# Sliding-window attention and a gated linear unit on one core: a rewrite with a fixed instruction order, 1 KB input rows and wider instructions

## The chip, the cores and the metric

The kernel runs on one core of a Trainium2 chip. The metric is the device time in microseconds of one execution, from the first to the last instruction of the core. The kernel before was timed three times: 296.49 us is the median, 295.57 and 297.37 are the ends. The profile shown here is a separate, recorded execution, whose span is 296.8 us.

## What is computed

There are 8 batches, 8 heads, 576 positions and 64 elements per head. Each position attends to at most 32 keys: heads 0 to 3 to the last 32 positions ("plain"), heads 4 to 7 to every fourth of the last 128 ("dilated"). The heads are joined to 512 channels, and a gated linear unit with a causal convolution of five taps follows.

```python
def _attn_ref(q, k, v):
    B, H, S, D = q.shape                      # 8, 8, 576, 64
    window, dilation = 32, 4
    scores = (1.0 / np.sqrt(D)) * np.matmul(q, k.transpose(0, 1, 3, 2))
    rel = pos[:, None] - pos[None, :]
    mask_plain = (rel >= 0) & (rel < window)
    mask_dil = (rel >= 0) & (rel < window * dilation) & (rel % dilation == 0)
    ...                                        # plain for h < H // 2, else dilated; softmax
    return np.matmul(attn, v)

def _moe_ref(x, w_val, conv_w, w_out):         # x: [8, 576, 512]
    ...                                        # xp: x with 4 zero rows ahead of each batch
    for k in range(K):                         # K = 5
        gate_pre += conv_w[k][None, None, :] * xp[:, k:k + S, :]
    gate = 1.0 / (1.0 + np.exp(-gate_pre))
    return gate * (x @ w_val) @ w_out
```

## The kernel before

Two heads make a pair, and a batch has four pairs, two plain and two dilated; 32 pairs in all. For each pair the kernel loads q, k and v, transposes q and k on TensorE (reading the upper halves of the fp32 words as bf16), computes the scores of blocks of 72 or 96 queries against 128 keys, takes the exponential on ScalarE, multiplies by a mask on VectorE, multiplies by v (with a column of ones that gives the sum), normalises, and transposes the result into `xT`, channels on partitions. The gated unit works on groups of 512 columns of `xT` and is put between the pairs. A scheduler orders the instructions of each engine.

```python
    # loads: one 256-byte row (64 fp32) per position and head
    for name, src in (("q", q), ("k", k)):
        t = inbuf.tile([KT, NKT, HPC, D], FP32, name=f"{name}_nat")      # KT = 96, NKT = 6, HPC = 2
        for hh in range(HPC):
            nc.sync.dma_start(out=t[:, :, hh, :],                          # line 186
                in_=src[b, h].rearrange("(t p) d -> p t d", p=KT))
    ...                                   # v, plain: three loads; dilated: eight loads, line 213

    # attn_pair
    for kt in range(NKT):
        nc.tensor.transpose(out=ps[:, kt * KT:(kt + 1) * KT],             # line 237
                            in_=src[:, kt, :, :], identity=ident_b[0:KT, 0:KT])
    if name == "q": nc.scalar.copy(out=dst, in_=ps)                       # line 244
    else:           nc.vector.tensor_copy(dst, ps)                        # line 246
    ...
    for grp in groups:                    # two halves of the blocks
        for hh in range(HPC):
            ps = ps_main.tile([128, 512], FP32, name="ps1")
            for bi in grp:
                nc.tensor.matmul(out=ps[0:klen, col:col + qlen],          # line 269
                    lhsT=kT[rb:rb + D, ucols(klo, klen, dil)],
                    rhs=qT[rb:rb + D, ucols(qlo, qlen, dil)], start=True, stop=True)
            nc.scalar.activation(out=et2[:, hh, g0:g0 + gcols],           # line 276
                in_=ps[:, 0:gcols], func=AF.Exp, scale=scale)
            nc.vector.tensor_tensor(out=et2[...], in0=et2[...],           # line 280
                in1=mask[:, g0:g0 + gcols], op=ALU.mult)
        for hh in range(HPC):
            for ci, bi in enumerate(grp):
                nc.tensor.matmul(out=ps[0:qlen, ci * AVS:ci * AVS + D + 1],   # line 288
                    lhsT=et2[0:klen, hh, offs[bi]:offs[bi] + qlen],       # 72 or 96 columns
                    rhs=v_bf[0:klen, bi, hh, 0:D + 1], start=True, stop=True)
            nc.vector.reciprocal(out=rec[0:QB, 0:na], in_=xv[0:QB, :, D])     # line 298
            nc.vector.tensor_tensor(out=xn[...], in0=xv[...], in1=rec[...])   # line 299
    ...                                   # transposes of xn, line 308
    if not dil: nc.vector.tensor_copy(dst_cols, xt_ps)                    # line 315
    else:       nc.vector.tensor_copy(dst_ap, src_ap)                     # line 323, written with a step of 4

    # gated unit: 10 groups of up to 512 columns, 4 channel blocks each
    def moe_group(c, grp):
        for kk in range(K):   nc.tensor.matmul(...)                       # line 331, conv_diag, 5 taps
        nc.scalar.activation(out=gate, in_=psg, func=AF.Tanh, scale=0.5)  # line 338
        for mc in range(NCH): nc.tensor.matmul(...)                       # line 342, w_val
        nc.vector.scalar_tensor_tensor(out=y_all[...], ...)               # line 348
    def moe_out_tile(b, t):               # five tiles of 128 (the last 64) positions per batch
        for c in range(NCH):  nc.tensor.matmul(...)                       # line 359, w_out
        nc.scalar.copy(out=osb, in_=pso)                                  # line 366
        nc.scalar.dma_start(out=out[b, bs0:bs0 + blen, :], in_=osb)
```

Of the kernel before, what the change touches and what calls it, by code (L numbers as in the profile page):

```python
# [24 lines left out]
def kernel(  # L26
# [10 lines left out]
    nc = tc.nc  # L37

# [3 lines left out]
    window = 32  # L42
    dilation = 4
    seg = S // dilation
    scale = 1.0 / float(D) ** 0.5

    KT = 96
    NKT = S // KT
    DT = seg // 2

    NCH = Dm // 128
    HPC = 128 // D
    NG = H // HPC

    SB = S + 4
    CB = B * SB
    GP = 512
    NGR = _ceil_div(CB, GP)

    KW = 128  # L60
    plain_blocks = []
    for t in range(NKT):
        qlo = t * KT
        klo = max(0, min(qlo - window, S - KW))
        plain_blocks.append((klo, KW, qlo, KT))
    dil_blocks = []
    for r in range(dilation):
        for x in range(2):
            qlo = r * seg + x * DT
            klo = max(r * seg, min(qlo - window, (r + 1) * seg - KW))  # L70
            dil_blocks.append((klo, KW, qlo, DT))

    def flat_offsets(blocks):
        offs, tot = [], 0
        for (_, _, _, qlen) in blocks:
            offs.append(tot)
            tot += qlen
        return offs, tot

    plain_offs, plain_tot = flat_offsets(plain_blocks)  # L80
    dil_offs, dil_tot = flat_offsets(dil_blocks)
    ET_COLS = max(plain_tot, dil_tot)
    NT_MAX = max(len(plain_blocks), len(dil_blocks))

    def head_cfg(dil):
        if dil:
            return dil_blocks, dil_offs, dil_tot, DT
        return plain_blocks, plain_offs, plain_tot, KT

    consts = ctx.enter_context(tc.tile_pool(name="consts", bufs=1))  # L90
    glob = ctx.enter_context(tc.tile_pool(name="glob", bufs=1))
    inbuf = ctx.enter_context(tc.tile_pool(name="inbuf", bufs=4))
    work = ctx.enter_context(tc.tile_pool(name="work", bufs=4))
    etbuf = ctx.enter_context(tc.tile_pool(name="etbuf", bufs=4))
    moe_sb = ctx.enter_context(tc.tile_pool(name="moe_sb", bufs=4))
    outbuf = ctx.enter_context(tc.tile_pool(name="outbuf", bufs=3))

    ps_tr = ctx.enter_context(tc.tile_pool(name="ps_tr", bufs=2, space=bass.MemoryType.PSUM))
    ps_main = ctx.enter_context(tc.tile_pool(name="ps_main", bufs=6, space=bass.MemoryType.PSUM))
    ps_moe = ps_main  # L100
    ps_sc = ps_main
    ps_av = ps_main

    ident_b = consts.tile([128, 128], BF16)
    nc.gpsimd.memset(ident_b, 0.0)
# [342 lines left out]
```

The softmax here doesn't subtract the row's maximum and nothing guards it: scores larger than these inputs give would overflow.

## Time and profile before

| engine | busy, us | share of the span | instructions |
|---|---|---|---|
| TensorE matmul | 219.5 | 74% | 2028 |
| TensorE weight load | 130.5 | 44% | 2028 |
| VectorE | 168.1 | 57% | 544 |
| ScalarE | 108.6 | 37% | 245 |
| GpSimd | 9.3 | 3% | 50 |

The core read 35.66 MB from memory and wrote 9.44 MB. The mean granted clock of TensorE was 0.853 of full speed. The busy time of an engine is what of the span one or more of its instructions cover. Where instructions overlap in the pipeline, the durations add up to more than the time they cover, so the pace of a run of matmuls is read from the distance between their starts. In the tables "x" is a count, and the text behind a bar names the idle time ahead of the group and what ended it.

### The profile page before, as it was taken

To read this page: it belongs to the slowest core of one execution; us is meant where nothing else is said; L and a number is where in the kernel's file an instruction comes from. 1 tells how busy PE (TensorE), PEld (TensorE's weight loads), DVE (VectorE), ACT (ScalarE), POOL (GpSimd) and SP (SyncE) were. 2 spreads that over 40 slices of the span, in tenths; PEclk is the share of its full clock that TensorE was granted. 3 is DMA by queue.
4 is the path that set the end of the run, shared out by engine and by line. 5 is a ranking of instruction groups with operands and counts; after the bars stand their busy time and mean duration, and the time that the engine had idled before them with its cause. 6 is when DMAs were issued, how large, how long until landed. Compare 5 with 4: busy or idle time off the path is not lost.

```text
span 296.8 us, 5724 instructions
## 1 busy us (share of the span) xinstructions
PE 219.5 (74%) x2028; PEld 130.5 (44%) x2028; DVE 168.1 (57%) x544; ACT 108.6 (37%) x245; POOL 9.3 (3%) x50
## 2 busy tenths in 40 slices
PE   1136559765798759785988488975978598879994
PEld 1125445454445445543555344543554355534441
DVE  0295666565647665765676464764576655655310
ACT  2022223422235522452345333542255225542253
POOL 9300000000000000000000000000000000000000
PEclk9999999955589958995799659995899559989998
DMA  7998899898500599749975699559975996540035
GB/s 207 253 176 174 149 203 161 182 205 156 93 0 35 161 207 181 151 150 177 202 153 148 168 208 155 130 156 195 192 147 175 175 190 121 160 111 0 2 141 177
DMA packets 142277, 45.47 MB, mean 153 GB/s; under 512 B 136613, under 2 KB 136613, under 8 KB 142250
## 3 DMA queue, kind: packets, MB, share of 16 engines
q1 hardware_dynamic: 135936, 33.57, 66.9%
q10 hardware_dynamic: 6314, 11.55, 11.2%
q8 instruction: 16, 0.26, 0.4%
q14 instruction: 11, 0.09, 0.1%
HBM read 35.66 MB, written 9.44 MB: 152 GB/s over the span
## 4 chain that ended last, share of the span: by engine, by line
PE 52%; DVE 14%; DMA 13%; SPq 13%; ACT 4%; issue 3%; DVEq 0%; ACTq 0%
PE ps L331 15%; PE ps L342 12%; PE ps L359 7%; DMA k_nat<-in_k_dram 6%; PE ps L288 6%; SPq L186 6%; PE ps L269 5%; DVE xT L323 4%; DMA out_dram<-out_sb 4%; SPq L213 4%; PE tr_ps L237 4%; DVE kT L246 4%; DVE y_all L348 3%; PE tr_ps L308 3%; SPq L205 2%
## 5 line engine op out<-in xcount | busy, mean ns | idle before, releaser
L288 PE MATMUL ps<-v_nat,et 128*72 128x65 bf16 (+1 forms) x448 | 50.0, 234 | 16.2 <-DVE et L280 15.3
L331 PE MATMUL ps<-xT,conv_diag 128*128 128x512 bf16 (+2 forms) x200 | 61.1, 406 | 0.0
L276 ACT ACTIVATE et<-ps 128x288 bf16<-128x288 f32 x128 | 42.2, 415 | 43.8 <-PE ps L269 43.8
L288 PEld LDWEIGHTS <-et 128*72 128x72 bf16 (+1 forms) x448 | 40.1, 147 | 37.3 <-DVE et L280 29.7
L280 DVE TENSOR_TENSOR et<-et,mask_flat 128x288 bf16<-128x288 bf16 x128 | 37.7, 299 | 30.5 <-ACT et L276 30.5
L348 DVE SCALAR_TENSOR_TENSOR y_all<-gate,ps 128x512 bf16<-128x512 bf16 (+2 forms) x40 | 25.3, 637 | 35.7 <-PE ps L342 30.1
L299 DVE TENSOR_TENSOR x_norm<-ps,recip 72x256 bf16<-72x256 f32 (+1 forms) x128 | 45.2, 376 | 0.2
L342 PE MATMUL ps<-xT,w_val_b 128*128 128x512 bf16 (+2 forms) x160 | 44.1, 386 | 0.4 <-DVE xT L323 0.4
L338 ACT ACTIVATE gate<-ps 128x512 bf16<-128x512 f32 (+2 forms) x40 | 22.2, 556 | 57.5 <-PE ps L331 57.5
L359 PE MATMUL ps<-w_out_b,y_all 128*128 128x512 bf16 (+1 forms) x160 | 42.1, 381 | 0.0
L244 ACT COPY qT<-tr_ps 128x576 bf16<-128x576 bf16 x32 | 20.4, 638 | 50.5 <-PE tr_ps L237 50.5
L269 PE MATMUL ps<-qT,kT 64*128 64x72 bf16 (+1 forms) x448 | 20.7, 244 | 20.1 <-DVE kT L246 17.7
L366 ACT COPY out_sb<-ps 128x512 f32<-128x512 f32 (+1 forms) x40 | 23.4, 585 | 27.2 <-PE ps L359 17.7
L237 PE MATMUL tr_ps<-ident_b,k_nat 96*128 96x96 bf16 x192 | 16.4, 233 | 19.5 <-DMA k_nat<-in_k_dram 9.7
L308 PE MATMUL tr_ps<-ident_b,x_norm 72*128 72x72 bf16 (+1 forms) x224 | 23.6, 228 | 8.9 <-DVE v_nat L192 8.3
L298 DVE RECIPROCAL recip<-ps 72x4 f32<-72x4 f32 (+1 forms) x128 | 20.9, 172 | 15.5 <-PE ps L288 13.3
L323 DVE COPY xT<-tr_ps 128x576 bf16<-128x576 bf16 x16 | 23.1, 1444 | 8.7 <-PE tr_ps L308 8.7
L269 PEld LDWEIGHTS <-kT 64*128 64x128 bf16 x448 | 15.0, 116 | 25.4 <-DVE kT L246 24.3
L246 DVE COPY kT<-tr_ps 128x576 bf16<-128x576 bf16 x32 | 14.6, 456 | 20.2 <-PE tr_ps L237 20.2
L308 PEld LDWEIGHTS <-x_norm 72*128 72x128 bf16 (+1 forms) x224 | 16.3, 112 | 21.3 <-DVE v_nat L192 11.0
L331 PEld LDWEIGHTS <-conv_diag 128*128 128x128 bf16 x200 | 18.7, 108 | 14.8 <-issue 3.3
L237 PE MATMUL tr_ps<-ident_b,q_nat 96*128 96x96 bf16 x192 | 17.0, 235 | 7.9 <-DMA q_nat<-in_q_dram 7.8
(26 smaller groups left out, 83.9 us busy)
## 6 DMA issues: line engine op xcount, KB each, us to landing
q_nat<-in_q_dram SPq DMA_DIRECT2D x64, 144.0 KB, 3.9
k_nat<-in_k_dram SPq DMA_DIRECT2D x64, 144.0 KB, 4.3
v_nat<-in_v_dram SPq DMA_DIRECT2D x144, 64.0 KB, 2.9
out_dram<-out_sb ACTq DMA_DIRECT2D x32, 256.0 KB, 2.2
v_nat<-in_v_dram SPq DMA_DIRECT2D x32, 160.0 KB, 4.1
w_stage<-in_moe_w_val_dram ACTq DMA_DIRECT2D x1, 1024.0 KB, 6.6
w_stage<-in_moe_w_out_dram ACTq DMA_DIRECT2D x1, 1024.0 KB, 10.6
out_dram<-out_sb ACTq DMA_DIRECT2D x8, 128.0 KB, 2.3
```

The costliest lines, as they stand in the source:

```text
L237: nc.tensor.transpose(out=ps[:, kt * KT:(kt + 1) * KT], in_=src[:, kt, :, :], identity=ident_b[0:KT, 0:KT],)
L269: nc.tensor.matmul(out=ps[0:klen, col:col + qlen], lhsT=kT[rb:rb + D, ucols(klo, klen, dil)], rhs=qT[rb:rb + D, ucols(qlo, qlen, dil)], st ...
L276: nc.scalar.activation(out=et2[:, hh, g0:g0 + gcols], in_=ps[:, 0:gcols], func=AF.Exp, scale=scale,)
L280: nc.vector.tensor_tensor(out=et2[:, hh, g0:g0 + gcols], in0=et2[:, hh, g0:g0 + gcols], in1=mask[:, g0:g0 + gcols], op=ALU.mult,)
L288: nc.tensor.matmul(out=ps[0:qlen, ci * AVS:ci * AVS + D + 1], lhsT=et2[0:klen, hh, offs[bi]:offs[bi] + qlen], rhs=v_bf[0:klen, bi, hh, 0:D ...
L299: nc.vector.tensor_tensor(out=xn[0:QB, b0:b0 + na, hh, :], in0=xv[0:QB, :, 0:D], in1=rec[0:QB, 0:na, None].to_broadcast([QB, na, D]), op=A ...
L308: nc.tensor.transpose(out=xt_ps[:, bi * QB:(bi + 1) * QB], in_=xn[0:QB, bi, :, :], identity=ident_b[0:QB, 0:QB],)
L323: nc.vector.tensor_copy(dst_ap, src_ap)
L331: nc.tensor.matmul(out=psg[:, lo:glen], lhsT=conv_diag[:, c, kk, :], rhs=xT[:, c, g0 + lo + kk - (K - 1):g0 + kk - (K - 1) + glen], start= ...
L342: nc.tensor.matmul(out=psv[:, lo:glen], lhsT=w_val_b[:, mc, c * 128:(c + 1) * 128], rhs=xT[:, mc, g0 + lo:g0 + glen], start=(mc == 0), sto ...
L348: nc.vector.scalar_tensor_tensor(out=y_all[:, c, g0 + lo:g0 + glen], in0=gate[:, lo:glen], scalar=1.0, in1=psv[:, lo:glen], op0=ALU.add, o ...
L359: nc.tensor.matmul(out=pso[0:blen, 0:Dm], lhsT=y_all[:, c, b * SB + 4 + bs0:b * SB + 4 + bs0 + blen], rhs=w_out_b[:, c, :], start=(c == 0) ...
```

## The change

The kernel is rewritten; what is computed stays. The order of the instructions of each engine is now the order of the program text, with no scheduler. The aims are fewer and larger DMA packets, fewer and longer instructions on VectorE and ScalarE, weight loads of always 128 columns, and matmuls of the gated unit placed where TensorE would wait.

- q and k (and v of dilated pairs) come in rows of four positions (1 KB). So a partition holds positions 4p to 4p+3, one of each residue class.
- Dilated pairs: each transpose takes two classes of one head (128 columns), still read as the upper bf16 halves. v is cast to bf16 on GpSimd.
- Plain pairs: GpSimd casts q and k to bf16 in the order class, head, element; eight transposes each follow. k is put back in position order by a ScalarE copy that reads PSUM with a step of 144 elements. q stays in class order.
- Scores of both heads go to two neighbouring PSUM banks; one exponential, one mask multiply, one reciprocal and one normalising multiply take both.
- The copy to `xT` goes to ScalarE for all pairs, and reads PSUM with the same step.
- `et` and `kT` are padded so that a weight load always takes 128 columns.
- Groups of the gated unit no longer run over the padding between batches; a group that crosses a batch border is done in two pieces. The output tiles are 36 of 128 positions.
- Weights come by a casting DMA of GpSimd, after the loads of the first pairs.

The core of the diff, cut:

```diff
+    ctx.enter_context(tc.manual_schedule(engines=None))
...
+    ps_s = ctx.enter_context(tc.tile_pool(name="ps_s", bufs=2, space=bass.MemoryType.PSUM))
+    ps_m = ctx.enter_context(tc.tile_pool(name="ps_m", bufs=4, space=bass.MemoryType.PSUM))
...
+        for name, src in (("q", q), ("k", k)):
+            rows = src[b, 2 * g:2 * g + 2].rearrange("h (p r) d -> p h (r d)", r=R)
+            a = inbuf.tile([P0, 2, R * D], FP32, name=f"{name}a")
+            nc.sync.dma_start(out=a, in_=rows[0:P0])
...
+    def convert(i):
+        if is_dil(i):
+            a, z, c0, c1 = nat[i]["v"]
+            for src, dst in ((a, c0), (z, c1)):
+                nc.gpsimd.tensor_copy(
+                    dst[:, :, :, 0:D], src.rearrange("p h (r d) -> p h r d", r=R))
+        else:
+            for name in ("q", "k"):
...
+                    nc.gpsimd.tensor_copy(
+                        c.rearrange("p r h d -> p h r d"),
+                        src.rearrange("p h (r d) -> p h r d", r=R))
...
+        if name == "k" and not is_dil(i):
+            nc.scalar.copy(out=dst[:, 0:S].rearrange("p (t r) -> p t r", r=R),
+                           in_=ps[:, 0:S].rearrange("p (r t) -> p t r", r=R))
+        else:
+            nc.vector.tensor_copy(dst[:, 0:S], ps[:, 0:S])
...
+        ps = ps_s.tile([128, 2, 512], FP32, name="sc")
...
+        nc.scalar.activation(out=et[:, :, 0:HALF], in_=ps[:, :, 0:HALF],
+                             func=AF.Exp, scale=scale)
...
+        nc.vector.tensor_tensor(out=ev, in0=ev, in1=for_mask, op=ALU.mult)
...
+                    nc.tensor.matmul(out=ps[:, x, c * DA:(c + 1) * DA],
+                                     lhsT=et[:, x, c * 96:c * 96 + 128],
+                                     rhs=vb[:, 3 * hf + c, x, :], start=True, stop=True)
...
+        nc.scalar.copy(out=xT[:, g, c0:c0 + S].rearrange("p (t r) -> p t r", r=R),
+                       in_=pv.rearrange("p r t -> p t r"))
...
+    groups = [(512 * j, 512) for j in range(7)] + [(3584, 448), (4032, 320), (4352, 256)]
...
+    def load_w(dst, src):
+        nc.gpsimd.dma_start(out=dst, in_=src.rearrange("(c p) n -> p c n", p=128))
...
+    COST = {"C": 1.1, "V": 0.9, "O": 0.9}
...
+    def fill(share):
+        budget[0] += share
+        while queue and budget[0] > 0.0:
+            budget[0] -= COST[queue[0][0]]
+            run_item()
...
+    transpose_in(0, "q")
+    transpose_in(0, "k")
+    per = 3.2
+    for i in range(n_steps):
+        b, g = order[i]
+        if i + 2 < n_steps:
+            load_qk(i + 2)
+            load_v(i + 2)
+            convert(i + 2)
+        if i == 0:
+            load_w(w_val_b, moe_w_val)
+        if i == 2:
+            load_w(w_out_b, moe_w_out)
+        scores(i, 0)
+        scores(i, 1)
+        fill(per * 0.35)
+        attn_v(i, 0)
+        if i + 1 < n_steps:
+            transpose_in(i + 1, "q")
+            transpose_in(i + 1, "k")
+        attn_v(i, 1)
+        fill(per * 0.65)
+        transpose_x(i)
+        if i < NCH:
+            conv_consts(i)
+        if i % NG == NG - 1:
+            for gi in group_ready.get(b, []):
+                add_group(gi)
+    while queue:
+        run_item()
```

In the new kernel a "step" is one pair. A unit of the gated unit is C (five convolution matmuls and a tanh), V (four value matmuls and the product) or O (four output matmuls, a copy and a store). `fill` takes units from a queue until a budget of 3.2 per step is used up.

## The prediction

> **What bounds the kernel now.** I read the page's slices first, then the windows of one batch, then the chain that ended last, then the groups.
>
> The slices (forty of 7.4 us; rows are busy tenths, granted TensorE clock, DMA share):
>
> ```profile
> PE   1136559765798759785988488975978598879994
> DVE  0295666565647665765676464764576655655310
> PEclk9999999955589958995799659995899559989998
> DMA  7998899898500599749975699559975996540035
> ```
>
> TensorE is never idle for long and never steadily full, its clock falls to half again and again, and the DMA engines go from nine tenths to nothing and back. It is a pattern with a period of 32 us, one batch. Four windows of 8 us show one period (matmul, weight load, VectorE, ScalarE, GpSimd busy with counts, granted clock, DMA share, GB/s):
>
> ```profile
> 104.00:112.00 8.00, 5.11 (x48) 3.54 (x49) 5.19 (x17) 1.96 (x5) 0.00 (x0) 0.50 1.27 207
> 112.00:120.00 8.00, 7.33 (x50) 3.83 (x48) 4.44 (x13) 2.43 (x4) 0.00 (x0) 0.87 1.08 171
> 120.00:128.00 8.00, 7.17 (x85) 4.49 (x86) 5.55 (x22) 4.39 (x12) 0.00 (x0) 1.00 0.70 148
> 128.00:136.00 8.00, 6.16 (x67) 3.56 (x66) 5.47 (x18) 4.16 (x9) 0.00 (x0) 0.91 0.48 147
> ```
>
> In the first window the DMA queues are full (207 GB/s), TensorE works 5.1 of 8 us, and all of it at half clock. Only in the other windows does TensorE run near full, with full clock. The chain says the same (share of the span by what it ran through):
>
> ```profile
> PE 52%; DVE 14%; DMA 13%; SPq 13%; ACT 4%; issue 3%; DVEq 0%; ACTq 0%
> ...
> 53.14 0.86 PE ps L342 x4
> 54.00 1.07 PE ps L331 x5
> ...
> 134.43 0.77 PE ps L288 x8
> 136.56 3.66 DMA k_nat<-in_k_dram
> ...
> 157.09 0.73 PE ps L269 x16
> ```
>
> So no one engine is the bound: half the span is TensorE work, a quarter is loads and their issue, the rest is hand-overs to VectorE. The chain also gives paces: a 512-column matmul takes 0.215 us (1.07/5, 0.86/4), a score matmul 0.73/16 = 0.045 us, a matmul with v 0.77/8 = 0.096 us. Six input transposes started 0.26 us apart from the next six at 87.4 us, 0.043 us each. The groups with the shapes kept apart give the weight loads and VectorE's costs:
>
> ```profile
> L288 PEld LDWEIGHTS <-et 128*96 128x96 bf16 x192 | 20.6, 160 | 18.8 <-DVE et L280 14.6 <-issue 3.1
> L269 PEld LDWEIGHTS <-kT 64*128 64x128 bf16 x448 | 15.0, 116 | 25.4 <-DVE kT L246 24.3 <-issue 1.2
> L323 DVE COPY xT<-tr_ps 128x576 bf16<-128x576 bf16 x16 | 23.1, 1444 | 8.7 <-PE tr_ps L308 8.7
> L280 DVE TENSOR_TENSOR et<-et,mask_flat 128x288 bf16<-128x288 bf16 x128 | 37.7, 299 | 30.5 <-ACT et L276 30.5
> L276 ACT ACTIVATE et<-ps 128x288 bf16<-128x288 f32 x128 | 42.2, 415 | 43.8 <-PE ps L269 43.8
> ```
>
> A load of 96 columns takes longer than one of 128, and a copy with a stepped output 1444 ns where the contiguous one of the same size takes 458.
>
> [...] 160 ns for 96 columns, 116 for 128. [...] the load queue's 135,936 packets, nearly all of 256 B, took 66.9% of 16 x 296.8 us, 23.4 ns each or 10.9 GB/s per engine; the other queue's 6,314 (11.55 MB) took 11.2%, 84 ns for 1,829 B on average, 21.8 GB/s. [...] Here 64 elements more cost the normalising multiply 63 ns (345 at 192, 408 at 256), so about 155 ns of each are fixed. [...]
>
> **The change part by part.**
>
> DMA. Before: 66.9% and 11.2% of the span, 232 us of all 16 engines. After: q and k 2 x 32 x 288 = 18,432 rows of 1 KB, dilated v 16 x 2 x 176 = 5,632; at an estimated 45 ns (half of the 84 ns, a little more) 24,064 x 45 / 16 = 68 us. Plain v stays at 24,576 of 256 B: 36 us. Output and weights 5,632 x 84 / 16 = 30 us. Sum 134 us, 100 less. At a step of under 6 us this is 4.2 us per step, no longer what one waits for. The load wait of some 3.5 us in each batch, and the half-clock window it makes, should go.
>
> VectorE, with the fixed cost: q copies 32 x 456 ns = 14.6 us; k copies of dilated pairs 16 x 456 = 7.3; mask multiplies 64 x (299 + 150) = 28.7; reciprocals 64 x 180 = 11.5; normalising 32 x 659 + 32 x 533 = 38.1; products 36 x 688 = 24.8; diagonals 3.3. Sum 128 us against 168. The largest single item is the copy to `xT` (23.1 + 7.3) that leaves.
>
> ScalarE gets it: exponentials 64 x (415 + 240) = 42; tanh 36 x 597 = 21.5; outputs 36 x 586 = 21; copies 48 x 638 = 31 if a stepped read costs no more than a contiguous one; stores some 13 us of issue. Sum 128 us against 109 + 15.
>
> GpSimd: 96 casts of 512 elements per partition. A memset grows from 179 to 205 ns between 96 and 128 columns, 0.8 ns per element; from that I take 0.6 to 1.0 us each, 60 to 95 us in all.
>
> TensorE at full clock, per step. Dilated: 12 x 43 + 16 x 45 + 16 x 45 + 8 x 43 ns = 2.3 us, where I give the matmul with v the pace of the score matmul, as both then load 128 columns (before 0.096; 448 x 0.05 = 23 us saved). Plain: 16 x 43 + 12 x 45 + 12 x 45 + 6 x 43 = 2.0. Mean 2.15. The gated unit: 4608 columns x 36 / 512 = 324 matmuls of 512 columns, plus 144 for the output, x 0.215 = 101 us. The pieces at borders cost little: five convolution matmuls of 32 columns start within 0.12 us at 287.0. A batch makes one group of 512 and four output tiles, (36 + 16) x 0.215 = 11.2 us, so 2.8 us per step, and 2.15 + 2.8 = 4.95.
>
> One wait I expect inside a step: after the last transposes ScalarE copies `xT` (0.64), then takes the first exponential (0.65), then VectorE masks (0.45), with some 0.4 for hand-overs: 2.1 us, while TensorE has both scores (0.6) and one unit (0.95) to do. It waits some 0.6 us; a second small one at the other half, 0.2. So a step takes 5.75 us, and TensorE is busy 86%, which by the windows above keeps its clock full.
>
> Sum. Start: before, weights were loaded with the first pair and the k transposes came at 13.3 us; now q and k of the first pair go first, some 7 us to its first scores. Pairs 0 to 3 have no gated work: by loads and hand-overs some 4.75 us each, 19 us. Steps 4 to 27: 24 x 5.75 = 138. Steps 28 to 31 use the full budget (3.1 + 2.15 + 0.8 = 6.05): 24. Left over: 101 - 6 x 11.2 - 12.4 = 21 us of gated work, and 3 us for the last copy and store (2.2 us to land). 7 + 19 + 138 + 24 + 24 = 212. I say 210, the waits being the softest term.
>
> **The rivals.**
>
> ScalarE becomes the bound. For it: a stepped output on VectorE cost three times the contiguous one, the new copies step through PSUM, and they stand ahead of the exponential that TensorE waits for. Against: here the read is stepped and the output contiguous. At 1.3 us a copy, 48 x 0.65 = 31 us more on ScalarE, of which the 28 copies to `xT` in the steady steps add some 0.6 each to the wait: about 228 us.
>
> [...]
>
> DMA stays the bound. If a 1 KB row cost four times a 256 B row (94 ns), loads and stores would take 141 + 36 + 30 = 207 us, and the time would be near 235. Against: the 84 ns of the longer packets.
>
> All waits hide. Then a step is TensorE's 4.95 and the sum about 190.
>
> **Range and chances.** The two extra costs seldom come in full together, and the paces of TensorE are measured, so the range is 188 to 238. To be slower than before, the steady steps would need over 8.5 us, more than any single engine's sum allows; only a fixed order that stalls at every hand-over could do that. Faster by over 2%: 0.94; within 2%: 0.02; slower: 0.04.
>
> **What would show it.** Right: DMA share under 0.7 in every steady window, clock near 1.0 from 30 us on, weight loads from `et` near 110 ns, q copies 456 ns, mask multiplies near 450, ScalarE copies near 640, VectorE busy near 128 us and ScalarE near 115, TensorE's largest idle in front of the matmuls with v, ended by the mask multiply, some 0.6 us a step. Wrong: copies to `xT` over 1 us; mask multiplies that vary in length or start late; half clock in steady windows; a steady DMA share near 1; or idle time in front of the input transposes of plain pairs, ended by GpSimd, which would mean that the casts set the pace.

## The result

The changed kernel takes 227.21 us (median; 225.51 to 229.44) and the kernel before 296.93 us in the same comparison: a ratio of 0.762, with a 95% interval of 0.757 to 0.768. The profiled execution spans 223.8 us at a mean granted clock of 0.992, against 296.8 us at 0.853 before. The predicted 210 us was 17 us too low; the range held.

The slices of the profile after (forty of 5.6 us, the same rows as before):

```profile
PE   2666689878988898898898898889888988999992
DVE  2566664775667556663666659656776566532320
PEclk9999999999999999996999999999999999999999
DMA  5799999747779799869989779778986300221232
```

TensorE is at seven to nine tenths from the sixth slice to the last but one, and one slice has lost clock, where before sixteen of the forty had. The DMA engines are busy until slice 31 and then fall off. Four windows of 8 us at the same places as before (columns as before):

```profile
104.00:112.00 8.00, 7.34 (x98) 5.83 (x96) 4.35 (x10) 3.46 (x7) 2.35 (x4) 0.91 1.09 237
112.00:120.00 8.00, 7.41 (x98) 5.43 (x97) 6.20 (x15) 3.12 (x6) 3.64 (x7) 1.00 0.85 218
120.00:128.00 8.00, 7.05 (x93) 4.40 (x91) 3.97 (x10) 5.54 (x10) 2.33 (x4) 1.00 0.83 241
128.00:136.00 8.00, 7.20 (x110) 6.15 (x108) 5.35 (x11) 4.04 (x8) 3.22 (x6) 1.00 0.79 208
```

The one-batch rhythm is gone: TensorE works 7.1 to 7.4 of 8 us in each. Before it was 5.1 to 7.3, and the first of those windows ran at half clock. The share of the DMA engines is 0.8 to 1.1 (1.09 in the first window; where it exceeds 1, the times of packets on one engine overlap), and from pair 3 to pair 27 TensorE waits for a load for 0.3 us in all. The chain that ended last:

```profile
PE 45%; DMA 15%; ACT 13%; DVE 10%; issue 7%; SPq 6%; ACTq 2%; POOL 0%; DVEq 0%
```

The groups that answer to those shown of before, shapes kept apart (busy us, mean ns, idle before and what ended it):

```profile
L246 PEld LDWEIGHTS <-et 128*128 128x128 bf16 x192 | 9.0, 101 | 11.2 <-DVE et L219 10.4
L197 PEld LDWEIGHTS <-kT 64*128 64x128 bf16 x448 | 11.2, 100 | 2.4 <-DVE kT L182 0.8
L278 ACT COPY xT<-bank 128x576 bf16<-128x576 bf16 x32 | 20.4, 637 | 23.1 <-PE bank L271 17.8 <-PE sc L197 2.9 <-PE bank L275 2.2
L219 DVE TENSOR_TENSOR et<-et,mask_d 128x576 bf16<-128x576 bf16 x32 | 16.7, 524 | 27.9 <-ACT et L212 26.9
L212 ACT ACTIVATE et<-sc 128x576 bf16<-128x576 f32 x64 | 38.5, 660 | 4.8 <-PE sc L197 4.8
...
L269 PE MATMUL bank<-ident_b,xn 96*128 96x96 bf16 x64 | 14.1, 221 | 4.4 <-DVE xn L256 4.4
L271 PE MATMUL bank<-ident_b,xn 48*128 48x48 bf16 x64 | 12.6, 197 | 0.0
```

Weight loads of `et` take 101 ns instead of 160. The copy to `xT`, read with a step on ScalarE, takes 637 ns; written with a step on VectorE it took 1444. L269 and L271, the transposes of dilated results, cover 26.7 us for 128 instructions, against 8.8 us for the 96 of the plain pairs. That is the largest surprise in this table.

**By stage.** I cut both profiled executions at the first score matmul and at the starts of the copies to `xT` of pairs 3, 27 and 31.

| stage | before, us | predicted, us | after, us |
|---|---|---|---|
| to the first scores | 14.5 | 7 | 6.9 |
| pairs 0 to 3 | 27.8 | 19 | 24.2 |
| steps 4 to 27, each | 8.02 | 5.75 | 5.97 |
| steps 28 to 31 | 34.8 | 24 | 23.9 |
| rest | 27.2 | 24 | 25.5 |

Two thirds of the gain, 24 x 2.05 = 49 us, lies in steps 4 to 27. There I split the time of a step in three: TensorE idle; the loss at half clock, estimated as half of what TensorE is busy at half clock; and the rest, which is TensorE's work at full clock. All runs below are cut in the same way. As half clock counts what the records show, and also the time before the first record, some 34 us here: the plain pairs' input transposes take 281 ns and start 0.080 us apart up to it, and 206 ns and 0.042 us after it, in every changed kernel. The clock row of the slices shows this stretch as full. In the half-clock stretches that are recorded in the kernel before, input transposes also take 281 ns and start 0.080 us apart.

| kernel | work, us per step | half-clock loss | idle | sum |
|---|---|---|---|---|
| before | 5.14 | 1.14 | 1.75 | 8.02 |
| after | 5.21 | 0.12 | 0.64 | 5.97 |
| regrouped transposes | 4.92 | 0.30 | 0.88 | 6.10 |
| `xT` copied on VectorE | 5.18 | 0.32 | 0.48 | 5.98 |
| weight loads of 96 columns | 5.39 | 0.17 | 0.59 | 6.15 |
| one bank at a time | 5.28 | 0.34 | 0.68 | 6.30 |
| with the scheduler | 5.47 | 0.09 | 0.54 | 6.10 |
| rows of 256 B | 5.27 | 0.66 | 1.55 | 7.48 |
| 336 loads of 1 KB rows | 5.23 | 0.26 | 0.82 | 6.31 |
| rotated order | 4.93 | 0.16 | 0.82 | 5.91 |
| rotated order, filled | 5.07 | 0.14 | 0.50 | 5.71 |

The executions profiled for "one bank at a time" (232.3 us) and "336 loads" (241.2 us) were slower than the medians of these runs (230.6 and 237.2), so these two rows show more loss than is typical.

The first two rows say where the gain came from. TensorE's work per step did not fall at all. The rewrite took away 1.1 us of idle time and 1.0 us of half clock in each step.

What ended TensorE's waits in the kernel before (whole execution: us, times, longest):

```profile
PE ps L269 <- DVE kT L246: 17.7, 30, 0.7
...
PE tr_ps L237 <- DMA k_nat<-in_k_dram: 9.7, 6, 5.5
PE tr_ps L237 <- DVE xT L323: 8.9, 11, 1.5
...
PE tr_ps L237 <- DMA q_nat<-in_q_dram: 7.8, 4, 6.5
```

The long waits for loads are those of the first pair. In steps 4 to 27 TensorE's 41.8 us of idle time before were 15.2 ahead of the scores (13.6 of them ended by the copy of k on VectorE), 10.8 ahead of the input transposes (6.3 ended by the copy to `xT`, 3.8 by loads), 9.2 ahead of the products with v and 6.7 ahead of the result transposes. After, the same four are 0.0, 0.0, 9.0 and 5.4 us. So what went stood ahead of the scores and the input transposes, and waits for loads were a small part of it.

### The profile page after: what moved, and what is told of

The parts are those of the page before. It is cut to its first block, busy times and chain, and to the rows that moved or that the text cites. A ratio compares the mean times of both kernels' runs of the same rounds, so it can differ in the third digit from the quotient of the medians.

```text
span 223.8 us, 5850 instructions
## 1 busy us (share of the span) xinstructions
PE 189.1 (85%) x2279; PEld 127.0 (57%) x2292; DVE 128.4 (57%) x311; ACT 108.7 (49%) x190; POOL 65.0 (29%) x123
## 3 DMA queue, kind: packets, MB, share of 16 engines
q1 hardware_dynamic: 52480, 30.95, 56.1%
q10 hardware_dynamic: 5194, 9.45, 11.8%
## 4 chain that ended last, share of the span: by engine, by line
PE 45%; DMA 15%; ACT 13%; DVE 10%; issue 7%; SPq 6%; ACTq 2%; POOL 0%; DVEq 0%
PE bank L303 16%; ACT et L212 9%; PE bank L315 8%; PE bank L329 5%; DVE et L219 4%; ACT osb L332 4%; DMA qa<-in_q_dram 4%; DVE xn L256 4%; DMA vp<-in_v_dram 3%; PE bank L269 3%; PE sc L246 2%; PE bank L271 2%; DMA ka<-in_k_dram 2%; ACTq L333 2%; DMA kzd<-in_k_dram 2%
## 5 line engine op out<-in xcount | busy, mean ns | idle before, releaser
L303 PE MATMUL bank<-xT,conv_diag 128*128 128x320 bf16 (+7 forms) x319 | 46.3, 295 | 0.3 <-DMA kzd<-in_k_dram 0.3
L256 DVE TENSOR_TENSOR xn<-sc,rec 96x512 bf16<-96x512 f32 (+1 forms) x64 | 39.7, 620 | 2.2
L212 ACT ACTIVATE et<-sc 128x576 bf16<-128x576 f32 x64 | 38.5, 660 | 4.8 <-PE sc L197 4.8
L307 ACT ACTIVATE gate<-bank 128x512 bf16<-128x512 f32 (+3 forms) x40 | 22.0, 556 | 32.8 <-PE bank L303 32.8
L315 PE MATMUL bank<-xT,w_val_b 128*128 128x320 bf16 (+7 forms) x254 | 37.1, 285 | 0.3 <-issue 0.3
L332 ACT ACTIVATE osb<-bank 128x512 f32<-128x512 f32 x36 | 21.6, 601 | 29.4 <-PE bank L329 23.4
L320 DVE SCALAR_TENSOR_TENSOR y_all<-gate,bank 128x512 bf16<-128x512 bf16 (+3 forms) x40 | 25.1, 628 | 18.0 <-PE bank L315 9.1
L303 PEld LDWEIGHTS <-conv_diag 128*128 128x128 bf16 x320 | 27.8, 100 | 12.6 <-issue 1.4
L329 PE MATMUL bank<-w_out_b,y_all 128*128 128x512 bf16 x134 | 33.7, 380 | 0.8 <-DVE y_all L320 0.2
L278 ACT COPY xT<-bank 128x576 bf16<-128x576 bf16 x32 | 20.4, 637 | 23.1 <-PE bank L271 17.8
L315 PEld LDWEIGHTS <-w_val_b 128*128 128x128 bf16 x256 | 20.8, 97 | 8.1
L179 ACT COPY kT<-bank 128x576 bf16<-128x576 bf16 x16 | 10.2, 638 | 20.4 <-PE bank L171 16.4
L246 PE MATMUL sc<-vp,et 128*128 128x65 bf16 x192 | 12.1, 201 | 7.5 <-DVE et L219 4.2
L269 PE MATMUL bank<-ident_b,xn 96*128 96x96 bf16 x64 | 14.1, 221 | 4.4 <-DVE xn L256 4.4
L236 PEld LDWEIGHTS <-et 96*128 96x128 bf16 x128 | 8.1, 100 | 14.1 <-DVE et L219 13.6
```

The source lines that it names most:

```text
L212: nc.scalar.activation(out=et[:, :, 0:HALF], in_=ps[:, :, 0:HALF], func=AF.Exp, scale=scale)
L236: nc.tensor.matmul(out=ps[:, x, hh * DA:(hh + 1) * DA], lhsT=et[0:96, x, hh * 96:hh * 96 + 128], rhs=c0[:, hh, r, :], start=True, stop=True)
L256: nc.vector.tensor_tensor(out=xo, in0=av[:, :, :, 0:D], in1=rec[:, :, 0:n, None].to_broadcast([96, 2, n, D]), op=ALU.mult)
L269: nc.tensor.transpose(out=pv[:, r, 0:96], in_=xn[:, 2 * r, :, :].rearrange("p h d -> p (h d)"), identity=ident_b[0:96, 0:96])
L278: nc.scalar.copy(out=xT[:, g, c0:c0 + S].rearrange("p (t r) -> p t r", r=R), in_=pv.rearrange("p r t -> p t r"))
L303: nc.tensor.matmul(out=ps[:, o:o + ln], lhsT=conv_diag[:, c, kk, :], rhs=xT[:, c, s:s + ln], start=(kk == 0), stop=(kk == K - 1))
```

## The experiments

Times are medians; ratios are to the kernel before in the same comparison, with 95% intervals. The edits are cut to their core. "After" stands at 0.762 (0.757 to 0.768).

**1. The dilated result transposes, regrouped.**

```diff
             for r in range(R):
                 nc.tensor.transpose(out=pv[:, r, 0:96], ...)      # 96 rows
+            for r in range(R):
                 nc.tensor.transpose(out=pv[:, r, 96:TT], ...)     # 48 rows
```

> The changed kernel (227.2 us), with the eight result transposes of a dilated pair in another order: first the four of 96 rows, then the four of 48. Theory: in the trace each of the eight starts 0.14 us after the one before, against 0.043 us for the six of a plain pair, because the row count changes each time; with one change in place of seven a pair saves 6 x 0.09 = 0.55 us of TensorE, 16 pairs 8.8 us, and since TensorE bounds the steps the time falls to 218 to 221 us. Rival: the distance comes from the transposes of 48 rows themselves, or from waiting for the normalised result; then the starts stay 0.14 us apart and the time stays within 1 us.

Measured: 229.02 us, ratio 0.771 (0.767 to 0.775). The groups, and the clock row of its slices:

```profile
L269 PE MATMUL bank<-ident_b,xn 96*128 96x96 bf16 x64 | 7.1, 214 | 7.4 <-DVE xn L256 7.4
L272 PE MATMUL bank<-ident_b,xn 48*128 48x48 bf16 x64 | 4.4, 186 | 0.0
...
PEclk9999999999999979995899979999999699999998
```

The transposes fell from 26.7 to 11.5 us, as expected, and work per step from 5.21 to 4.92 us. Yet the kernel became no faster. Idle time ahead of L269 rose from 4.4 to 7.4 us, because TensorE now arrives earlier at the same normalised results, and half clock came back in four places (17 us in all, of which 13.7 in steps 4 to 27). What was saved on TensorE was paid out as waiting and as clock. This made the order of the instructions, and not the amount of work, the thing to look at.

**2 and 3. Do loads set the pace?** First the weights two pairs later, to relieve the DMA engines at the start (in the changed kernel their share is 1.0 to 1.2 from 12 to 32 us):

```diff
-        if i == 0: load_w(w_val_b, moe_w_val)
-        if i == 2: load_w(w_out_b, moe_w_out)
+        if i == 2: load_w(w_val_b, moe_w_val)
+        if i == 4: load_w(w_out_b, moe_w_out)
```

> The changed kernel with the loads of w_val and w_out issued two pairs later (at pairs 2 and 4 in place of 0 and 2). Theory: the first four pairs are bound by their loads (DMA share over 1.0 from 8 to 32 us), among which the 1 MB of w_val costs some 4 us; pair 3 is done 2 to 4 us sooner and the time falls by as much, to 223 to 225 us. Rival: the first pairs are bound by hand-overs between engines, and the time stays within 1 us.

Measured: 228.83 us, ratio 0.765 (0.760 to 0.771); pair 3 comes at 31.5 us, not earlier. But the share from 12 to 24 us stayed at 1.2, so this edit relieved the start little. Then v is loaded only for the first dilated and the first three plain pairs. This leaves out the other loads of v (10.5 of 41.8 MB), and later pairs are multiplied by the v that is there.

```diff
+            if cnt["d"] == 0:              # dilated: only the first pair loads v
                 nc.sync.dma_start(out=once["a"], in_=rows[0:96]) ...
+            if cnt["p"] > NVP: return      # plain: only the first three
```

> The changed kernel without most loads of v: the first dilated and the first three plain pairs load v, the others compute with what is there (10.5 of 41.8 MB are left out). Theory (TensorE bounds the steady steps): pairs 0 to 3 gain 2 to 5 us, the steps after them under 0.1 us each, in all 222 to 226 us. Rival (the loads, with a DMA share near 0.8, pace the steps): a step falls from 5.97 us to 5.3 or less, and the time to 210 us or less.

Measured: 228.27 us, ratio 0.770 (0.766 to 0.774), 6.00 us per step, pair 3 at 31.6 us. A quarter of the bytes is worth nothing in the steady steps. For the start the run says less, as of the first six pairs only the second and the sixth do without their loads of v. The trace of the changed kernel says more: from the first scores to pair 3's copy (24.2 us) TensorE is idle for 7.8 us, of which it waits 0.2 for loads and 0.6 for casts, and busy for 16.4 at half clock, with one pair at a time and no gated work beside it.

**4. Rows of 256 B again**, for q and k of plain pairs and v of dilated pairs, by giving the rows in SBUF a pad; these loads are issued per head.

```diff
-            a = inbuf.tile([P0, 2, R * D], FP32, name=f"{name}a")
-            nc.sync.dma_start(out=a, in_=rows[0:P0])
+            a = inbuf.tile([P0, 2, R, DP], FP32, name=f"{name}a")       # DP = 66
+            for hh in range(2):
+                nc.sync.dma_start(out=a[:, hh, :, 0:D], in_=rr[0:P0, hh])
```

> The changed kernel with the q and k of plain pairs and the v of dilated pairs again in 256-byte packets (14,848 rows of 1 KB become 59,392 of 256 B), everything else equal but four more load instructions per pair. By the mean packet times of the trace (60 ns and 21.3 ns) the DMA engines get 14,848 x 25 ns / 16 = 23 us more to do. Theory (TensorE bounds): a DMA share near 0.95, and 1 to 6 us more, mostly in pairs 0 to 3. Rival (loads pace): 12 to 25 us more, 240 to 252 us.

Measured: 277.38 us (269.94 to 283.53; too wide for a ratio). That is 50 us slower by the medians and 44 by the fastest of each kernel (269.94 and 225.51), far outside what either side expected. The chain:

```profile
SPq 29%; PE 28%; DMA 24%; ACT 6%; issue 6%; POOL 3%; DVE 2%; ACTq 1%; POOLq 0%; DVEq 0%
```

SyncE's queue, which starts the loads, leads it. Its timeline (start, us, what, count):

```profile
111.04 1.24 SPq L124 DMA_DIRECT2D va<-in_v_dram  x2
112.31 1.27 SPq L126 DMA_DIRECT2D vz<-in_v_dram  x2
114.01 1.23 SPq L104 DMA_DIRECT2D qa<-in_q_dram  x2
115.29 1.26 SPq L112 DMA_DIRECT2D qzp<-in_q_dram  x2
116.65 1.24 SPq L104 DMA_DIRECT2D ka<-in_k_dram  x2
```

One start follows the other, 0.6 us each. Over the run it starts 336 loads at 0.578 us with 0.059 us between, 214 us; with 19.5 us of waits that makes 233 us, which is when the last load is started. A step has 10.5 loads; at 0.64 us these are 6.7 us, with the waits 7.3, and the step takes 7.48. The packets themselves are hardly the reason: those of this queue took 49.7% of 16 x 268.2 us, or 133 us, against 56.1% of 223.8, or 126 us, with long rows. So the steps follow the queue, which was busy starting loads for 214 of 233 us. TensorE feels it through the casts (waits: total us, times, longest):

```profile
PEld L183 <- POOL kcz L155: 11.3, 14, 2.2
PEld L179 <- POOL kca L155: 10.7, 10, 2.1
```

In the changed kernel neither of these pairs has more than 1 us. But the run changed two things, the rows and the number of loads, so:

**5. The same 336 loads with rows of 1 KB.**

```diff
-            nc.sync.dma_start(out=a, in_=rows[0:P0])
+            for hh in range(2):
+                nc.sync.dma_start(out=a[:, hh:hh + 1], in_=rows[0:P0, hh:hh + 1])
```

> The changed kernel with its rows of 1 KB, but with as many load instructions as the run with rows of 256 bytes: the loads of q, k (plain pairs) and v (dilated pairs) are split by head, 336 loads instead of 240. Theory (the run with short rows was slow because SyncE starts one load after the other and takes about 0.7 us for each, 10.5 per pair or 7.3 us, more than a pair's 6 us): 255 to 285 us, SyncE's queue starting loads without a break until about 235 us, steps of 7.2 to 7.6 us. Rival (the short rows themselves, by their packets, made it slow): 225 to 233 us, steps of 5.9 to 6.2 us.

Measured: 237.22 us, ratio 0.796 (0.791 to 0.800), 6.31 us per step. This lies between the two expectations. A start takes 0.464 us here, the waits sum to 27 us, and the last load is started at 201 us. So the number of loads alone costs 10 us, and the remaining 34 to 40 us of run 4 came with the short rows. The 192 loads whose rows differ between the two runs take SyncE 0.64 us each in run 4 and 0.44 in run 5. Over all 336 starts that is a mean of 0.58 instead of 0.46 us, or 38 us more on the one queue that was already full. Whether the row length itself or the pad in SBUF makes these starts longer is not separated: the 48 loads of plain v, with rows of 256 B in both runs, took 0.51 and 0.47 us. The changed kernel has 240 starts of 0.487 us, 117 us, with 44 us of waits before the last one at 174 us: slack, but not much.

**6. The copy to `xT` on VectorE.**

```diff
-        nc.scalar.copy(out=xT[...], in_=pv.rearrange("p r t -> p t r"))
+        nc.vector.tensor_copy(xT[...], pv.rearrange("p r t -> p t r"))
```

> The changed kernel with the copy to xT on VectorE again (same operands, stepped read of PSUM), 32 copies. Theory: VectorE gets 32 x 0.75 us = 24 us more (152 in place of 128 of 224 us), ScalarE 20 us less; as the copy no longer stands ahead of the first exponential, the wait of TensorE for the first masked exponential gets shorter, so 0 to 8 us faster. Rival (VectorE is the scarcer engine, or a stepped read costs it over 1.4 us as the stepped write did): 3 to 15 us slower.

Measured: 226.74 us, ratio 0.753 (0.751 to 0.756). Idle time falls to 0.48 us per step, since the exponential no longer stands behind the copy, and its profiled execution pays 0.32 us of half clock per step. By the ratios it is about 1% faster than the changed kernel, with intervals that all but touch.

**7. Weight loads of 96 columns** ahead of the products with v:

```diff
-   out=ps[:, x, c * DA:(c + 1) * DA],    lhsT=et[:, x, c * 96:c * 96 + 128]
+   out=ps[0:96, x, c * DA:(c + 1) * DA], lhsT=et[:, x, c * 96:c * 96 + 96]
```

> The changed kernel with weight loads of 96 in place of 128 columns ahead of the 448 matmuls with v. Theory (fast loads of 128 columns are worth what the prediction said): a load goes from 100 to 140 ns or more, the matmuls with v start 0.07 to 0.09 us apart in place of 0.035, 448 x 0.045 = 20 us of TensorE, of which some lies in waits: 10 to 20 us slower. Rival: the loads hide beside the matmuls; within 3 us.

Measured: 233.54 us, ratio 0.782 (0.778 to 0.786). One of its groups:

```profile
L246 PEld LDWEIGHTS <-et 128*96 128x96 bf16 x192 | 12.7, 135 | 10.3 <-DVE et L219 9.4 <-issue 0.5
```

The loads take 135 instead of 101 ns, the products start 0.045 instead of 0.033 us apart, and the kernel loses 6 us. The direction is as expected and the size smaller: the starts moved by 0.012 us, where 0.035 to 0.055 were expected, and 6 us were lost instead of 10 to 20.

**8. The counterpart in the kernel before: loads of 128 columns.** For this `et2` becomes a tile per half, with 8 buffers in place of 4, and GpSimd sets its pad.

```diff
-                        lhsT=et2[0:klen, hh, offs[bi]:offs[bi] + qlen],
+                        lhsT=et2[0:klen, hh, offs[bi] - g0:offs[bi] - g0 + 128],   # et2 padded, per half
```

> The kernel before, with the weight loads ahead of the products with v taking 128 columns (et padded), everything else as it was. Theory (a load of fewer than 128 columns costs these matmuls their pace, 0.096 us from start to start instead of 0.03 to 0.045; 368 of them, of which the part on the path counts): the pace falls below 0.05 us and the kernel gains 5 to 9 us, 288 to 292 us. Rival (the time saved becomes a longer wait for VectorE): pace the same gain, time within 2 us of before.

Measured: 295.80 us, ratio 0.993 (0.991 to 0.996).

```profile
L289 PE MATMUL ps<-v_nat,et 128*128 128x65 bf16 x448 | 44.9, 220 | 17.6 <-DVE et L281 17.0 <-DMA v_nat<-in_v_dram 0.2
L289 PEld LDWEIGHTS <-et 128*128 128x128 bf16 x448 | 29.8, 112 | 42.5 <-DVE et L281 32.3 <-issue 4.7
```

TensorE's busy time fell by 10.3 us (219.5 to 209.2), and its idle time rose by 5.1 in the profiled execution. By the medians, 2 us arrived, as the rival said. But the theory's premise was wrong. Its 0.096 us come from eight products at 134.43 us, of which all but the first three started at half clock (it fell at 134.53 us), with a wait of 0.15 us among them. At full clock the products with v that follow one another start 0.042 us (96 columns) and 0.037 us (72) apart in the kernel before, and 0.034 us in this run. There was little to gain, so the run does not show what a large gain in pace would have bought.

**9. One bank at a time**: exponential, mask, reciprocal and normalising multiply twice, for one head each.

```diff
-        nc.scalar.activation(out=et[:, :, 0:HALF], in_=ps[:, :, 0:HALF], func=AF.Exp, scale=scale)
+        for x in range(2):
+            nc.scalar.activation(out=et[:, x, 0:HALF], in_=ps[:, x, 0:HALF], func=AF.Exp, scale=scale)
```

> The changed kernel with the exponential, mask multiply, reciprocal and normalising multiply done once per PSUM bank again (256 more instructions in all). VectorE gets 64 x (0.15 + 0.17 + 0.155) = 30 us more, ScalarE 64 x 0.09 = 6 us more. Theory (TensorE bounds, the others have slack but stand in its waits): each of the two waits of a step grows by 0.1 to 0.2 us, 5 to 12 us slower. Rival 1: the smaller pieces hand over sooner, and it is 0 to 5 us faster. Rival 2 (VectorE is near its bound): 20 to 30 us slower.

Measured: 230.57 us, ratio 0.766 (0.763 to 0.769), with VectorE busy 145.7 instead of 128.4 us. The ratio is 0.0035 above that of the changed kernel, 1 us. The durations of VectorE's instructions add up to 32 us more, as expected; where they overlap, its busy time rises by 17 us, and even that is nearly all hidden.

**10. The scheduler instead of the fixed order.**

```diff
-    ctx.enter_context(tc.manual_schedule(engines=None))
```

> The changed kernel with the order of the instructions left to the scheduler, which also ordered the kernel before. Theory (the placing of the units fills waits of TensorE that a scheduler leaves open): 10 to 40 us slower, with TensorE's idle time growing from 31 us. Rival (the gain is in the smaller work of the engines and not in the order): within 5 us.

Measured: 230.63 us, ratio 0.774 (0.770 to 0.777). First scores come at 9.2 us and pair 3 at 35.0 us (31.1 after); the steps take 6.10 us. TensorE's idle time did not grow: 0.54 us per step against 0.64. The order as it was fixed is worth 3 to 4 us, about what is lost up to pair 3. My theory gave it far more.

**11 and 12. Another fixed order.** The runs so far say that TensorE's work is near 5 us per step and that what is left is short waits. Both products with v of pair i go first, then the transposes of q and k of pair i + 2 while VectorE normalises, then the scores of pair i + 1, the transposes of the result, and the gated unit, which covers exponential and mask. The regrouping of run 1 is in.

```diff
+        attn_v(i, 0); attn_v(i, 1)
+        transpose_in(i + 2, "q"); transpose_in(i + 2, "k")
+        scores(i + 1, 0); scores(i + 1, 1)
+        transpose_x(i)
+        fill(per)                       # the whole share of the gated unit
```

> The changed kernel in another fixed order, with the regrouped transposes: both products with v of a pair first, then q and k of the pair after next are transposed while VectorE normalises, then the scores of the next pair, then the transposes of the result, then all of the gated unit's share, which covers the exponential and the mask. Loads go one pair further ahead. Theory (TensorE's short waits inside a pair, 15 us in steps 4 to 27, and one pair's latency of 5.3 us per step at the start can be hidden by order alone): idle time of steps 4 to 27 falls from 15 to 3 to 8 us, the first pairs take about 4.3 us each, 207 to 216 us in all. Rival (the granted clock takes back what is gained, as in the regrouped run): 222 to 229 us with 15 us or more at half clock. Second rival (ScalarE or VectorE become the bound because each now works in bursts): 219 to 230 us with TensorE's waits on masks or copies above 15 us.

Measured: 228.77 us, ratio 0.769 (0.766 to 0.773). After its first rise, at 43.6 us, the clock never fell, so the first rival is out; but idle time rose to 20 us in steps 4 to 27. It stands ahead of the scores, which wait for the normalising multiplies of the pair before (waits of this run):

```profile
PEld L197 <- DVE xn L256: 25.3, 49, 1.2
```

The start lost as well: pair 3 comes at 33.5 us. I put this down to q and k of pair 2, which are transposed ahead of pair 0's result and must have been loaded and cast. So in the last run one unit of the gated share went ahead of the scores, and the first four pairs transpose only the next pair:

```diff
+        if early: transpose_in(i + 1, ...)  # between the two products with v
+        else:     transpose_in(i + 2, ...); fill(per * 0.35)
         scores(i + 1, 0); scores(i + 1, 1)
         transpose_x(i)
+        fill(per * 0.65)                # per, whole, after pair 3
```

> The rotated order mended at the three places where the rotated run lost: a third of the gated unit's share (about one unit, 1.1 us) now stands ahead of the scores, where TensorE waited for the normalising multiplies (0.3 to 0.5 us ahead of each half's scores); in the first four pairs q and k of the next pair only are transposed, between the two products with v, so that no work waits for loads of a pair further ahead; the rest of the share follows the transposes of the result. Theory (those waits were order alone): idle time of steps 4 to 27 falls from 20 to 3 to 9 us, steps of 5.2 to 5.5 us, pair 3's copy at 29 to 31 us, 207 to 216 us in all. Rival (half clock comes back and takes what is gained): 219 to 227 us with 10 us or more at half clock in steps 4 to 27. Second rival (the waits only move, to ScalarE's and VectorE's work of the gated unit ahead of exponential and mask): idle time above 15 us, now ahead of the products with v, 222 to 230 us.

Measured: 215.23 us (214.94 to 215.51), ratio 0.720 (0.717 to 0.723). This beats the changed kernel by 12 us. Pair 3 comes at 30.1 us, the steps take 5.71 us, idle time is 12.1 us. The first five of these steps, with the change from one order to the other, average 7.5 us, with 1.2 us idle, and the other 19 about 5.3, with 0.3 us idle. Its slices:

```profile
PE   1567879979599999999999899989999999998992
PEclk9999999999969999999999999999999999999998
```

Time was at the upper end of what the theory gave, and idle time above it (3 to 9 us): between 31 and 175 us, 3.9 us stand ahead of the products with v, 3.1 ahead of the scores and 3.1 ahead of the input transposes. The regrouping of run 1, which alone gained nothing, is part of this run; the order was not run without it.

## Why the prediction was right, and what it had wrong

**The cause.** It said that the load wait of each batch and the half-clock window that this wait makes should go, and that a step would be TensorE's work plus some 0.8 us of waits. Both went, and the 49 us of the gain that lie in the steady steps are half idle time and half clock. But the account of them was wrong, and that the number came out is in part luck.

- Waits for loads were 4.4 of the 41.8 us that TensorE was idle in the steady steps before. What went were mainly the 15.2 us ahead of the scores and the 10.8 ahead of the input transposes, which the prediction put together as "hand-overs to VectorE" and gave no reason to go.
- The load wait did not bring on the half-clock window, though it may have lengthened it. The clock fell first: at 134.5 us, with the waits for q and k ending at 138.8 and 140.3; likewise at 165.3, 199.4 and 230.1 us, with waits ending at 172.2, 203.5 and 236.3. In the kernel before, after the clock's first rise, six stretches of 10 to 23 us have no matmul of the gated unit, and in each the clock fell 2.6 to 3.7 us after it began. In the changed kernel, once the gated unit has begun, the longest such stretch is 3.7 us. So I put the clock's part of the gain down to the gated unit being spread over all steps (the last section has the figures); no run undid this alone.

TensorE's part was wrong in its terms. The products with v were to start 0.045 us apart instead of 0.096 and to save 23 us; but 0.096 was a half-clock pace (run 8), and the step is from about 0.04 to 0.033 us. Per step, at full clock (each matmul counts until the next one starts or it ends, and half at half clock):

| TensorE's work, us per step | before | predicted | after |
|---|---|---|---|
| input transposes | 0.73 | 0.60 | 0.74 |
| scores | 0.47 | 0.63 | 0.38 |
| products with v | 0.69 | 0.63 | 0.46 |
| result transposes | 0.30 | 0.30 | 0.74 |
| gated unit | 2.93 | 2.80 | 2.90 |

What scores and products with v gained against the kernel before, 0.33 us, the new dilated result transposes used up.

**The sum.** It was 212 us, and the profiled span is 223.8. The 11.8 us are:

- Pairs 0 to 3: 24.2 instead of 19 us, 5.2 more. The term "some 4.75 us each" was taken "by loads and hand-overs", with TensorE at full clock in mind. It was not the loads: TensorE waited 0.8 us for loads and casts there. It was busy for 16.4 us at half clock, half of which, 8.2 us, is the estimated loss: more than the whole error. Part was order too, as run 12 took 22.9 us here with 6.3 us of idle time.
- Steps 4 to 27: 5.97 instead of 5.75 us, 24 x 0.22 = 5.4 more. Work is 0.26 over, half clock 0.12, idle 0.16 under. The most mis-sized term is "8 x 43 ns" for the dilated result transposes. They started 0.14 us apart, 1.1 us for eight, as 96 and 48 rows alternate. With them the result transposes are 0.44 us over, the input transposes 0.14 and the gated unit 0.10; scores and products with v, faster than charged, give 0.42 back. Run 1 shows that grouping by row count takes the term away (work 0.29 us less).
- The rest: 25.5 instead of 24 us. First scores (6.9 for 7) and steps 28 to 31 (23.9 for 24) were right.

**DMA.** "An estimated 45 ns" for a 1 KB row was wrong: the 24,064 such packets took 60 ns on average (median 46, so some took far longer). All packets took 158 us of 16 engines, not 134, and the share in steady windows was 0.8 to 1.1, not under 0.7. I had listed "a steady DMA share near 1" as a sign of being wrong. It wasn't one: run 3 takes a quarter of the bytes away and gains nothing. A busy DMA engine is not a wait. Nor was it always the engines that paced the loads of the kernel before: six times SyncE's queue stood still for 5.5 to 23.7 us, as a load there waits for a semaphore that an output store raises (waits of SyncE in the kernel before):

```profile
SPq L213 <- DMA out_dram<-out_sb: 57.7, 7, 23.7
```

In the longest, a load of v had its turn at 76.8 us and started at 100.5, when a store that ScalarE had issued at 98.4 us landed; from 80 to 88 us the DMA share was 0.01. Four rows of 256 B cost 4 x 18.5 = 74 ns in run 4 against 60 for one of 1 KB, so the long rows were worth less on the DMA engines than I said and, by run 4, more on SyncE, whose starts the prediction never summed.

**Engines.** VectorE was busy for 128.4 us. The 128 that I said was a sum of durations, and these came to 139 (mask multiplies 33.8 instead of 28.7), so that the two agree is luck. GpSimd 65.0 us (60 to 95), ScalarE 118 us of durations, 108.7 busy, without its issue of stores (115), exponentials 660 ns (655), stepped copies 637 ns (638), `et` loads 101 ns (110), q copies 444 ns (456). The longest of TensorE's idle time was ahead of the matmuls with v, ended by the mask multiply, as said (waits of the changed kernel; the weight load waits first):

```profile
PEld L236 <- DVE et L219: 13.6, 18, 1.3
PEld L246 <- DVE et L219: 10.4, 10, 1.6
...
PEld L269 <- DVE xn L256: 5.2, 8, 0.7
```

In steps 4 to 27 the matmuls with v account for 9.0 of TensorE's 15.4 us of idle time, 0.37 us a step, less than the 0.6 and 0.2 predicted. The other 5.4 us stand ahead of the result transposes, a wait that the prediction did not list.

**The rivals.** ScalarE as the bound fell: a stepped read of PSUM cost it nothing extra (637 ns against 638 for the contiguous copy before), and run 6, which relieves it, gains about 1%. DMA as the bound fell with run 3. "All waits hide" did not happen; in run 12 another order halved the idle time in its last 19 steps (0.32 us). Mask multiplies that vary in length, listed as a sign of being wrong, are there: the 20 that overlap a cast on GpSimd take 677 ns on average and the other 44 take 460. Nothing more on how the two engines meet is shown, and it is 4.3 us of VectorE's time in all (20 x 0.217), of which only a part is on the path.

**What stays open.** Undone one at a time, the parts cost little: by the ratios the fixed order 3.5 us, two banks in one instruction 1, wide weight loads 6, the copies to `xT` nothing. The loads (number and rows together) cost 44 to 50. These are not shares of the 70 us gained, since each was measured where the others had left slack. The casts on GpSimd and the two classes per transpose were not undone. Which part ended the waits ahead of the scores is not shown; it is not the fixed order alone, as with the scheduler idle time and half clock stay low (0.54 and 0.09 us per step). Nor is it shown what spreading the gated unit is worth by itself, or how much of the start's 8 us large matmuls ahead of the first pair would save.

## What to carry to other kernels

Split a step into work, half-clock loss and idle time before choosing what to change: here the busiest engine's work stayed as it was, and the regrouped transposes with an order that put large matmuls ahead of the dependent steps gave 12 us more. Look at which came first before calling one loss the cause of another: here the clock fell before the wait that was blamed for it. Read a pace only where the clock is full: input transposes started 0.080 us apart at half clock and 0.042 at full. Count the load instructions on their queue (number x duration of a start) as an engine of its own, beside bytes and packets, and see what that queue waits for. An engine's saved time counts only if the next instruction was ready: the regrouped transposes saved 0.29 us of work per step and bought nothing in the first order.

## What the runs showed of the hardware that I had not expected

**Which matmuls hold the clock.** The records give the clock as full (1.00) or half (0.50), and inside the runs each half-clock stretch is a multiple of 3.41 us: in the kernel before one, three, four or seven times, in the changed kernel once. Six of the full stretches of the kernel before last 20.48 us, six times as long. I therefore laid a grid of 3.41 us through each of the 14 traces, aligned to its first drop, and took, from each window at recorded full clock up to 15 us before the end, the share that the gated unit's large matmuls cover:

| gated unit's share of the window | windows | clock halved right after |
|---|---|---|
| under 0.15 | 32 | 31 |
| 0.15 to 0.3 | 44 | 13 |
| 0.3 to 0.5 | 162 | 0 |
| over 0.5 | 434 | 0 |

How busy TensorE was does not order the windows in this way. In the changed kernel's one drop (at 102 us) it was busy 82% of the window ahead of it, with transposes, scores and products with v; the gated unit had 10%. Another 70 windows had TensorE busy under 80% but a gated share over 0.3, and none was followed by a drop. So in these traces the small matmuls of the attention did not hold the clock by themselves (with a gated share under 0.15 it halved after 31 of 32 windows), and the share by which the prediction expected full clock, TensorE busy 86%, is not the one that the drops follow. The start fits: in all 14 traces the clock first became full 1.7 to 5.5 us after the first matmul of the gated unit (at 33.7 us after 32.0 in the changed kernel, at 49.2 after 45.6 before), however much of the attention had run until then. This is read from traces, with the grid aligned to the drops; no run changed only this, and the traces do not tell which property of the large matmuls counts.

**Alternating row counts.** Transposes of 96 and of 48 rows in turn start 0.14 us apart. In two groups they start 0.025 to 0.05 us apart, and only the one change between the groups takes 0.14 (run 1). Plain ones, all of 96 rows, start 0.043 us apart.

**Starting a load.** SyncE starts one load after the other. The same 192 loads took it 0.44 us each with 1 KB rows and 0.64 us with 256 B rows into a padded tile (runs 5 and 4).

**A packet's time varies between kernels.** 256 B packets took 23.8 ns on average in the kernel before, 21.3 ns in the changed one, 18.5 and 18.1 ns in runs 4 and 5, and 25.9 ns in run 3, which has them only at its crowded start. That crowding is the reason is not shown.
